# A two-stream attention block: the scale weight in two column chunks, the value rows in single key tiles, the last blocks of the value product moved

## The chip, the cores and the metric

The kernel runs on one core of a Trainium2 chip. The time is the device time in microseconds (us) of one execution. TensorE (PE in the profile) multiplies and transposes, and its weight loads are listed apart as PEld; VectorE (DVE), ScalarE (ACT) and GpSimd (POOL) work elementwise; SyncE (SP) issues most of the loads, and 16 DMA engines carry them out. The core's own work runs in program order on each engine, and the engines wait for one another through semaphores.

## The reference

Two streams of tokens, image (2 batches of 256) and text (2 of 32), with a model width of 1152, are normed, modulated by a vector `c`, projected to query, key and value, attended to together, projected and gated. Everything is bfloat16 at the borders.

```python
mod_i = (silu(c) @ wmod_img).reshape(B, 6, 1, D)     # the same for the text stream
shi, sci, gai = mod_i[:, 0], mod_i[:, 1], mod_i[:, 2]
hi = layernorm(x_img) * (1 + sci) + shi
qkvi = hi @ wqkv_img                                 # query, key, value
...
p = softmax(einsum('bqd,bkd->bqk', q, k) * D ** -0.5)
a = einsum('bqk,bkd->bqd', p, v)
out_i = x_img + gai * (a[:, Nt:] @ wo_img)
out_t = x_txt + gat * (a[:, :Nt] @ wo_txt)
```

What matters here is the first stage: the norm of the image tokens, the factor `1 + sci`, the value part of `hi @ wqkv_img`, and the shift `shi`.

## The kernel before

The width of 1152 is nine tiles of 128, called kt. The 512 image tokens are four blocks of 128, called i or x0 to x3; x0 and x1 belong to batch 0, x2 and x3 to batch 1. All engines follow the order in which the program is written: the schedule is manual, so an instruction that waits holds up everything behind it on its engine.

**Loads.** SyncE issues, in this order, the token blocks (`load_x`, L90) and the two weight matrices of the stage in chunks (`load_sc`, L94, and `load_v`, L98). The scale weight `w_sc_i` is cut by output columns, in chunks of 2, 2, 2 and 3 tiles (`KC`, L49): a chunk holds all 1152 rows of 256 or 384 columns, so that each piece of a row in a load is 512 or 768 bytes. The value weight `w_v_i` is cut by rows, in the same groups of kt, with whole rows of 2304 bytes. Behind these come the shift weight `w_sh_i` and the query weight `w_q_i`.

**Start.** TensorE runs 11 matmuls on zeros (`warm`, L127) while the first loads arrive. VectorE norms each block (`stats_of`, `std_of`, `out_of`; the square root between them is ScalarE's, L160). TensorE transposes the normed block in nine steps (`x_transposes`, L172) into two PSUM tiles, and ScalarE copies these to `hT_i`, the transposed tokens: plain copies (`evac_low`, `evac_high`) for the kt whose factor is not there yet, and copies multiplied with the factor (`evac_scaled`, L181) for those whose factor is.

**The factor.** `mod_scale` (L198) multiplies one column chunk of the scale weight with `silu(c)`: nine matmuls of two columns for each of its tiles. ScalarE or VectorE adds 1 and writes `mod_i`. For the kt that were copied without the factor, `apply_mod` (L208) multiplies `hT_i` in place on VectorE (0), GpSimd (1) or ScalarE (2).

**The value product.** `v_part` (L229) adds one chunk of kt to one accumulator: one block i and one half of 512 of the first 1024 value columns. Seven of the eight accumulators are open at once, in the seven PSUM banks of the pool `ps_mm`, which the transposes also use; an eighth bank is the pool `ps_sm`. Chunk 0 of all blocks comes first, then chunk 1, 2 and 3, with the transposes of x2 and x3 and the factors of chunks 1 to 3 between them. After the last chunk an accumulator is copied to `v_i` by `evac`, which takes VectorE and ScalarE in turn.

**The end of the stage.** `v_rest` (L336) computes the last 128 value columns for two blocks, once for x2, x3 and once for x0, x1. `rows_for_cols` (L369, with `strip_rows`, L357) multiplies the shift weight with `silu(c)` into four strips of rows; `select_cols` and `cols_out` turn these into columns. The eighth accumulator (x3, columns 512 to 1023; L390 to L395) is computed around this: four of its matmuls ahead of `select_cols` and five behind it. Then `apply_mod` adds the shift to `hT_i` in place (L397 to L399), and the query products start (`qk_img`, L441). The shift must come behind all the value products, because these use `hT_i` without it.

Of the kernel before, what the change touches and what calls it, by code (L numbers as in the profile page):

```python
# [14 lines left out]
def kernel(  # L15
# [33 lines left out]
    KC = [(0, 2), (2, 4), (4, 6), (6, KT)]  # L49
# [42 lines left out]
    def load_sc(ch):  # L92
        k0, k1 = KC[ch]
        nc.sync.dma_start(w_sc_i[:, :, k0 * P:k1 * P], w_view(wmod_img)[:, :, D + k0 * P:D + k1 * P])  # L94

    def load_v(ch):
        k0, k1 = KC[ch]
        nc.sync.dma_start(w_v_i[:, k0:k1, :], w_view(wqkv_img)[:, k0:k1, 2 * D:3 * D])  # L98
# [3 lines left out]
    load_sc(0)  # L102
    load_x(2)
    load_v(0)
    load_x(3)
    for ch in range(1, len(KC)):
        load_sc(ch)
        load_v(ch)
# [63 lines left out]
    def x_transposes(i, n0=5):  # L172
        tps = (ps_mm.tile([P, n0, P], bf, tag="mm", name="tp"),
               ps_mm.tile([P, KT - n0, P], bf, tag="mm", name="tp") if n0 == 5 else
# [6 lines left out]
    def evac_scaled(i, tps, n):  # L181
        for kt in range(n):
# [3 lines left out]
    def evac_low(i, tps, n):  # L186
        nc.scalar.copy(hT_i[:, n:tps[2], i * P:(i + 1) * P], tps[0][:, n:tps[2], :])
# [4 lines left out]
    def mod_cols(wt, out_ps, j0, j1):  # L192
        for j in range(j0, j1):
            for kt in range(KT):
                nc.tensor.matmul(out_ps[:, j - j0, :], lhsT=wt[:, kt, j * P:(j + 1) * P], rhs=sT[:, kt, :],
                                 start=(kt == 0), stop=(kt == KT - 1))

    def mod_scale(ch, eng, own=True):  # L198
        k0, k1 = KC[ch]
        pool, tag = (ps_sm, "sm") if own else (ps_mm, "mm")  # L200
        mps = pool.tile([P, KT, B], f32, tag=tag)
        mod_cols(w_sc_i, mps, k0, k1)
        if eng == "dve":
            nc.vector.tensor_scalar_add(mod_i[:, KT + k0:KT + k1, :], mps[:, 0:k1 - k0, :], 1.0)
        else:
            nc.scalar.activation(mod_i[:, KT + k0:KT + k1, :], mps[:, 0:k1 - k0, :], ACT.Identity, bias=1.0)
# [22 lines left out]
    def v_part(i, half, ch):  # L229
        k0, k1 = KC[ch]  # L230
        if ch == 0:
# [7 lines left out]


    def v_block(units, chs):
        for ch in chs:
            for (i, half) in units:
                v_part(i, half, ch)

    warm(4)
    silu_c()
    warm(7)
# [10 lines left out]

    stats_of(0, 0, NCH)  # L260
# [5 lines left out]
    evac_low(0, tps, 2)  # L266
# [42 lines left out]
    for (i, half) in SEVEN[:4]:  # L309
        v_part(i, half, 2)  # L310
# [532 lines left out]
```

## Time and profile before

| | us |
|---|---|
| median of 3 runs | 117.31 (117.13 to 117.89) |
| span of the profiled execution, first to last instruction | 115.8 |
| the median less that span | 1.5 |
| first scale matmul (L195) starts | 7.68 |
| first value matmul (L235) starts | 9.95 |
| last scale chunk's matmuls start | 20.26 |
| first query matmul (L450) starts | 32.47 |
| TensorE busy over the span | 110.6 |

Only the span of the profiled execution is known, not its time outside; the table sets the median beside it. In the profile, a line such as `L235 PE MATMUL va<-w_v_i,hT_i ... x63` names the source line, the engine, the operation, what is written from what, and how many instructions. The chain of waits follows the end of the kernel back, step by step, to what released each step. A time to landing counts from the issue of a load on its queue to the arrival of its last byte. A busy TensorE is not a TensorE at its peak, since matmuls overlap; where pace matters, the distance between starts is used. The granted clock is full throughout.

### The profile page before, as it was taken

How to read it: one execution, taken by the hardware profiler on the slowest of the kernel's cores; microseconds unless marked ns; L12 is line 12 of the kernel's file. 1: busy time of each engine (PE TensorE's matmuls, PEld its weight loads, DVE VectorE, ACT ScalarE, POOL GpSimd, SP SyncE). 2: the span in 40 equal slices, each digit the busy share in tenths (PEclk: the TensorE clock that was granted, in tenths of full speed). 3: DMA queues.
4: the chain of work that ended last, by engine and by line, in shares of the span. 5: the costliest groups of instructions: out<-in, count | busy, mean ns of one | idle time of the engine just before them, and what ended most of it. 6: DMA issues, size and time to landing. Idle time of an engine off the chain costs nothing.

```text
span 115.8 us, 2947 instructions
## 1 busy us (share of the span) xinstructions
PE 110.6 (96%) x1262; PEld 65.3 (56%) x1262; DVE 53.7 (46%) x138; ACT 34.2 (30%) x83; POOL 24.0 (21%) x55
## 2 busy tenths in 40 slices
PE   5978999999999999999999999999999999999990
PEld 1344563548644444486444445987677665568570
DVE  1689920354290312211572332136665804994771
ACT  4548660343270320121080121116455700000200
POOL 4000103660050000002215000000240300999000
PEclk9999999999999999999999999999999999999999
DMA  3999999999999999999999999999999999982052
GB/s 83 297 338 359 376 385 399 409 412 415 404 408 408 413 412 400 414 410 294 375 404 411 396 376 381 404 412 402 412 408 405 404 416 410 409 297 108 6 187 68
DMA packets 22840, 40.89 MB, mean 353 GB/s; under 512 B 1183, under 2 KB 6699, under 8 KB 22827
## 3 DMA queue, kind: packets, MB, share of 16 engines
q1 hardware_dynamic: 22032, 39.82, 91.8%
q0 software_dynamic: 480, 0.73, 1.7%
q8 instruction: 10, 0.16, 0.5%
q10 hardware_dynamic: 315, 0.14, 0.5%
q14 instruction: 3, 0.02, 0.1%
HBM read 39.36 MB, written 1.34 MB: 351 GB/s over the span
## 4 chain that ended last, share of the span: by engine, by line
PE 80%; SPq 9%; DMA 8%; issue 1%; DVE 1%
PE qkps L450 30%; PE ps L762 15%; DMA w_sc_i<-in_wmod_img_dram 8%; PE va L235 5%; SPq L98 5%; PE aps L671 5%; PE ps L507 4%; PE sps L531 4%; PE gps L361 4%; SPq L90 3%; PE ops L783 2%; PE ps L395 2%; PE ps L340 2%; PE ps L603 2%; SPq L94 1%; PE gps L423 1%
## 5 line engine op out<-in xcount | busy, mean ns | idle before, releaser
L450 PE MATMUL qkps<-hT_i,t 128*128 128x512 bf16 x162 | 35.6, 379 | 0.0
L450 PEld LDWEIGHTS <-t 128*128 128x128 bf16 x162 | 15.6, 98 | 18.6
L762 PE MATMUL ps<-t,aT 128*128 128x384 bf16 x99 | 16.4, 326 | 0.0
L762 PEld LDWEIGHTS <-aT 128*128 128x128 bf16 x117 | 11.1, 98 | 6.7 <-issue 0.2
L235 PE MATMUL va<-w_v_i,hT_i 128*128 128x512 bf16 x63 | 14.6, 379 | 0.2 <-ACT hT_i L183 0.2
L746 POOL TENSOR_TENSOR w_og<-t,gb 128x384 bf16<-128x384 bf16 x9 | 8.7, 996 | 6.1 <-DMA gb<-mod_scratch 6.1
L235 PEld LDWEIGHTS <-hT_i 128*128 128x128 bf16 x63 | 5.8, 97 | 6.8 <-ACT hT_i L190 0.3
L768 DVE TENSOR_TENSOR tmp<-ps,gb 128x384 bf16<-128x384 f32 x11 | 6.0, 549 | 4.9 <-DMA gb<-mod_scratch 4.2
L434 DVE TENSOR_SCALAR qkT<-qkps 128x512 bf16<-128x512 f32 x4 | 2.8, 692 | 11.4 <-PE qkps L450 11.4
L153 DVE BATCH_NORM_STATS2 stats<-x_i 128x6 f32<-128x384 bf16 x12 | 6.0, 542 | 2.6 <-DMA x_i<-in_x_img_dram 2.6
L130 PE MATMUL wps<-wz 128*128 128x512 bf16 x14 | 5.9, 574 | 1.2 <-DVE wz L120 1.2
L436 ACT ACTIVATE qkT<-qkps 128x512 bf16<-128x512 f32 x5 | 2.9, 596 | 13.6 <-PE qkps L450 13.6
L144 DVE CAST qkT<-qkps 128x512 bf16<-128x512 f32 x4 | 2.8, 692 | 6.7 <-PE qkps L450 6.7
L219 POOL TENSOR_SCALAR hT_i<-hT_i,mod_img 128x256 bf16<-128x256 bf16 x5 | 2.5, 510 | 16.1 <-ACT rstd L160 9.6
L146 ACT CAST qkT<-qkps 128x512 bf16<-128x512 f32 x5 | 2.8, 582 | 9.7 <-PE qkps L450 9.7
L558 POOL DMA_DIRECT2D mod_scratch<-g_sb x2 | 1.2, 583 | 20.7 <-ACT g_sb L556 20.7
L769 DVE TENSOR_TENSOR o<-tmp,x_i 128x384 bf16<-128x384 bf16 x11 | 5.2, 471 | 0.4
L684 DVE TENSOR_SCALAR aT<-aps,sv 128x288 bf16<-128x288 f32 (+2 forms) x11 | 4.3, 456 | 2.3 <-PE aps L671 2.3
L507 PEld LDWEIGHTS <-t 128*128 128x128 bf16 x162 | 4.9, 98 | 0.2
L507 PE MATMUL ps<-hT_t,t 128*128 128x64 bf16 x162 | 4.9, 193 | 0.0
L738 ACT CAST gbf_full<-bps 128x288 bf16<-128x288 f32 x2 | 0.7, 402 | 14.2 <-PE bps L736 14.2
L671 PE MATMUL aps<-pT,v_i 128*128 128x288 bf16 (+2 forms) x44 | 4.8, 264 | 0.1
(156 smaller groups left out, 139.8 us busy)
## 6 DMA issues: line engine op xcount, KB each, us to landing
t<-in_wmod_img_dram SPq DMA_DIRECT2D x2, 2592.0 KB, 19.3
t<-in_wqkv_img_dram SPq DMA_DIRECT2D x6, 864.0 KB, 13.8
t<-in_wqkv_txt_dram SPq DMA_DIRECT2D x2, 2592.0 KB, 18.4
t<-in_wmod_txt_dram SPq DMA_DIRECT2D x2, 1440.0 KB, 15.0
t<-in_wqkv_txt_dram SPq DMA_DIRECT2D x3, 864.0 KB, 16.0
t<-in_wmod_txt_dram SPq DMA_DIRECT2D x1, 2592.0 KB, 19.5
t<-in_wo_txt_dram SPq DMA_DIRECT2D x3, 864.0 KB, 15.3
t<-in_wmod_txt_dram SPq DMA_DIRECT2D x2, 1152.0 KB, 16.2
```

The costliest lines, as they stand in the source:

```text
L98: nc.sync.dma_start(w_v_i[:, k0:k1, :], w_view(wqkv_img)[:, k0:k1, 2 * D:3 * D])
L130: nc.tensor.matmul(ps[:], lhsT=wz[:, 0:P], rhs=wz[:], start=True, stop=True)
L153: nc.vector.bn_stats(stats[0:np_, k, :], x_ap[:, k * CH:(k + 1) * CH])
L235: nc.tensor.matmul(ps[:], lhsT=hT_i[:, kt, i * P:(i + 1) * P], rhs=w_v_i[:, kt, half * VW:(half + 1) * VW], start=(kt == 0), stop=(kt == K ...
L361: nc.tensor.matmul(gps[32 * g:32 * g + 32, 0:RC], lhsT=lhs[:, kt, :], rhs=wt[:, kt, g * RC:(g + 1) * RC], start=(kt == 0), stop=(kt == KT ...
L450: nc.tensor.matmul(pss[j - j0][:], lhsT=wq[:, kt, j * P:(j + 1) * P], rhs=hT_i[:, kt, :], start=(kt == 0), stop=(kt == KT - 1))
L507: nc.tensor.matmul(ps[:, j - j0, :], lhsT=wq[:, kt, j * P:(j + 1) * P], rhs=hT_t[:, kt, :], start=(kt == 0), stop=(kt == KT - 1))
L671: nc.tensor.matmul(bank[:, off:off + c1 - c0], lhsT=lhsT, rhs=rhs, start=(first[id(bank)] == n), stop=(final[id(bank)] == n))
L746: nc.gpsimd.tensor_mul(w_og[:, dt, 0:CH], w_o_i[:, dt, NG0:D], gb[:, B - 1, NG0:D])
L762: nc.tensor.matmul(ps[:, 0:cw], lhsT=aT[:, dt, t0:t0 + P], rhs=rhs, start=(dt == DTS[0]), stop=(dt == DTS[-1]))
L768: nc.vector.tensor_mul(tmp[:, 0:cw], ps[:, 0:cw], gb[:, b, cs])
L769: nc.vector.tensor_add(o[:, cs], tmp[:, 0:cw], x_i[:, i, cs])
```

## The change

The scale weight is now cut into two column chunks, of 4 and 5 tiles, and each chunk is loaded in two halves by rows (5 and 4 kt), so that a piece of a row is 1024 or 1280 bytes. The value weight is loaded in pieces of 1, 1, 2, 1, 2 and 2 kt instead of 2, 2, 2 and 3. There are 14 loads in this stage instead of 12.

`mod_half` runs the matmuls of one half of a chunk; two halves add up in one PSUM tile, and `mod_out` adds 1. The first chunk gives the factor of kt 0 to 3 at once, so `evac_scaled` covers four kt of each block, and only kt 4 to 8 are multiplied in place later, all in one go behind the second chunk. The square roots of x2 and x3 stand behind three scaled copies of the block before. `v_rows` runs the value matmuls kt by kt, both halves of a block together: kt 0 and 1 of x0 now come ahead of the transposes of x1, kt 2 and 3 of x0 and kt 0 and 1 of x1 ahead of those of x2, and so on. One warm-up pair stands between the two halves of the first chunk, one behind it (four instead of three in all). The last five kt are run unit by unit at the end.

At the end of the stage, the eighth accumulator is computed whole and copied out ahead of the shift rows; the narrow block of x2, x3 comes between the shift rows and `select_cols`, and that of x0, x1 behind `cols_out`, with its copy to `v_i` behind the shift.

```diff
-    KC = [(0, 2), (2, 4), (4, 6), (6, KT)]
+    KA = 4
+    KC = [(0, KA), (KA, KT)]
+    KH = [(0, 5), (5, KT)]
...
+    def load_sc(ch, half):
+        c0, c1 = KC[ch]
+        k0, k1 = KH[half]
+        nc.sync.dma_start(w_sc_i[:, k0:k1, c0 * P:c1 * P], w_view(wmod_img)[:, k0:k1, D + c0 * P:D + c1 * P])
+
+    def load_v(k0, k1):
         nc.sync.dma_start(w_v_i[:, k0:k1, :], w_view(wqkv_img)[:, k0:k1, 2 * D:3 * D])
 
     load_x(0)
     load_x(1)
-    load_sc(0)
+    load_sc(0, 0)
+    load_sc(0, 1)
+    load_v(0, 1)
     load_x(2)
-    load_v(0)
+    load_v(1, 2)
     load_x(3)
-    for ch in range(1, len(KC)):
-        load_sc(ch)
-        load_v(ch)
+    load_v(2, 4)
+    load_sc(1, 0)
+    load_sc(1, 1)
+    load_v(4, 5)
+    load_v(5, 7)
+    load_v(7, KT)
...
+    def mod_half(ch, half):
+        c0, c1 = KC[ch]
+        k0, k1 = KH[half]
+        if half == 0:
+            mod_ps[ch] = ps_sm.tile([P, KT, B], f32, tag="sm", name="mps")
+        for kt in range(k0, k1):
+            for j in range(c0, c1):
+                nc.tensor.matmul(mod_ps[ch][:, j - c0, :], lhsT=w_sc_i[:, kt, j * P:(j + 1) * P], rhs=sT[:, kt, :],
+                                 start=(kt == 0 and j == c0), stop=(kt == KT - 1 and j == c1 - 1))
...
+    def v_rows(i, k0, k1, halves=(0, 1)):
+        for kt in range(k0, k1):
+            for half in halves:
+                v_part(i, half, kt, kt + 1)
...
     tps = x_transposes(0)
     stats_of(1, 1, NCH)
-    evac_low(0, tps, 2)
+    evac_high(0, tps)
     std_of(1)
-    mod_scale(0, "act")
-    evac_scaled(0, tps, 2)
-    evac_high(0, tps)
+    mod_half(0, 0)
+    warm(2)
+    mod_half(0, 1)
+    mod_out(0, "act")
+    evac_scaled(0, tps, 0, KA)
     out_of(1)
-    warm(3)
+    warm(2)
+    v_rows(0, 0, 2)
     tps = x_transposes(1)
     stats_of(2, 0, NCH)
-    evac_scaled(1, tps, 2)
+    evac_scaled(1, tps, 0, 3)
     std_of(2)
-    evac_low(1, tps, 2)
+    evac_scaled(1, tps, 3, KA)
     evac_high(1, tps)
     stats_of(3, 0, 1)
     out_of(2)
-    v_block([(0, 0), (0, 1), (1, 0), (1, 1)], [0])
+    v_rows(0, 2, KA)
+    v_rows(1, 0, 2)
     tps = x_transposes(2, KT - 1)
     stats_of(3, 1, NCH)
-    evac_scaled(2, tps, 2)
+    evac_scaled(2, tps, 0, 3)
     std_of(3)
...
+    evac_scaled(2, tps, 3, KA)
     evac_high(2, tps)
+    evac_low(2, tps)
     out_of(3)
+    v_rows(1, 2, KA)
+    v_rows(2, 0, 2)
     tps = x_transposes(3, KT - 1)
     evac_high(3, tps)
+    evac_scaled(3, tps, 0, KA)
+    evac_low(3, tps)
+    v_rows(2, 2, KA)
+    mod_half(1, 0)
+    mod_half(1, 1)
+    mod_out(1, "dve")
+    for kt in range(*KC[1]):
+        apply_mod(kt, 0, TPB, False, 0 if kt < KT - 1 else 2)
+        apply_mod(kt, TPB, NIT, False, 1 if kt < KT - 1 else 2)
+    v_rows(3, 0, KA, (0,))
     v_i = act.tile([P, NIT, D], bf, tag="A")
...
+    for (i, half) in [(i, half) for i in range(NIT) for half in range(2)][:7]:
+        v_part(i, half, KA, KT)
...
-    v_rest(TPB, NIT)
-    v_rest(0, TPB)
+    ps = ps_mm.tile([P, VW], f32, tag="mm")
+    for kt in range(KT):
+        nc.tensor.matmul(ps[:], lhsT=hT_i[:, kt, 3 * P:4 * P], rhs=w_v_i[:, kt, VW:NM], start=(kt == 0), stop=(kt == KT - 1))
+    evac(v_i[:, 3, VW:NM], ps[:])
     shr = rows_for_cols(w_sh_i, "shr")
     cps = ps_sm.tile([P, NCOL + B], f32, tag="sm")
-    ps = ps_mm.tile([P, VW], f32, tag="mm")
-    for kt in range(KT):
-        if kt == 4:
-            select_cols(shr, cps)
-            cols_out(mod_i[:, 0:KT, :], cps, 0.0)
-        nc.tensor.matmul(ps[:], lhsT=hT_i[:, kt, 3 * P:4 * P], rhs=w_v_i[:, kt, VW:NM], start=(kt == 0), stop=(kt == KT - 1))
+    v_rest_out(TPB, NIT, v_rest(TPB, NIT))
+    select_cols(shr, cps)
+    cols_out(mod_i[:, 0:KT, :], cps, 0.0)
+    vr = v_rest(0, TPB)
...
-    evac(v_i[:, 3, VW:NM], ps[:])
+    v_rest_out(0, TPB, vr)
```

## The prediction

> **What bounds the kernel now.** I read the page's chain first, then the chain of waits of the first 33 us, then the timelines of TensorE and ScalarE there, and last the load issues one by one.
>
> ```profile
> span 115.8 us, 2947 instructions
> ...
> PE 80%; SPq 9%; DMA 8%; issue 1%; DVE 1%
> ```
>
> And the chain in order of time (start, length, what ran):
>
> ```profile
> 11.42 8.79 DMA w_sc_i<-in_wmod_img_dram
> 20.21 0.05 issue
> 20.26 0.83 PE mps L195 x27
> 21.09 6.00 PE va L235 x27
> 27.09 2.01 PE ps L340 x36
> 29.09 1.10 PE gps L361 x36
> ...
> 32.47 17.48 PE qkps L450 x81
> ```
>
> From 20.26 us on the chain is TensorE almost without a break. Whatever moves the start of the query products (32.47 us) moves the end equally; no later wait on a load would absorb it. The span is 115.8 us; the median of the runs, 117.31, is 1.5 us more, which I carry unchanged.
>
> The chain names a DMA until 20.21 us, but that overstates the loads: TensorE was working until just before, by its timeline (start, length, engine, line, what):
>
> ```profile
> 9.10 0.68 PE L178 MATMUL tp<-ident,xn_i 128*128 128x128 bf16 x9 [0.15 <-DVE xn_i L165]
> 9.95 1.89 PE L235 MATMUL va<-w_v_i,hT_i 128*128 128x512 bf16 x8 [0.17 <-ACT hT_i L183]
> 11.90 0.68 PE L178 MATMUL tp<-ident,xn_i 128*128 128x128 bf16 x9
> 12.41 0.59 PE L195 MATMUL mps<-sT,w_sc_i 128*128 128x2 bf16 x18
> ...
> 16.58 3.61 PE L235 MATMUL va<-w_v_i,hT_i 128*128 128x512 bf16 x16
> ```
>
> Steady prices: 16 value matmuls in 3.61 us, of which the last is pipeline: 0.217 each (27 in 6.00 later: 0.222); nine transposes 0.52 before the next may start (11.90 to 12.41); a scale matmul 0.026 (18 in 0.59). From 9.10 TensorE had 27 transposes (1.6), 63 value matmuls (13.7), 63 scale matmuls (1.6), 36 narrow ones (2.1), the shift rows (1.3), and the last wide block with its selection (2.2): 22.5 us, so 31.6; the end was 32.47, so all waits in this stretch are below 0.9 us. That is the most that better loads can win.
>
> **The loads** (x0 to x3 are the four token blocks, value row k the k-th 128 rows of the value weights). Issue plus time to landing, one load at a time: x1 lands at 4.5 us, scale chunk 0 at 7.7, x2 at 8.3, value chunk 0 at 9.8, x3 at 10.6, scale 1 at 12.2, scale 2 at 15.3, scale 3 at 20.2, value 3 at 22.3. Two of the answers (scale chunk 0 and value 3; the last column is us to landing):
>
> ```profile
> w_sc_i<-in_wmod_img_dram SPq DMA_DIRECT2D x1, 576.0 KB, 6.0
> ...
> w_v_i<-in_wqkv_img_dram SPq DMA_DIRECT2D x1, 864.0 KB, 10.4
> ```
>
> From 7.7 to 22.3 us 5.31 MB landed. The 3.25 MB with 2304-byte rows take 7.9 us at the 411 GB/s of the stretch 22 to 24 us, which leaves 6.7 us for 2.06 MB of short scale rows (512 and 768 bytes): 306 GB/s. The new scale rows are 1024 and 1280 bytes; their rate lies between 306 and 411, and I take 360, the middle. At 306 GB/s chunk 0 should take 1.9 us behind x1; it took 3.2. This opening lag of 1.25 us is still 1.0 at scale 1 and 0.7 at scale 2 by the same sums.
>
> New order after x1 (0.59 MB at 4.5): scale half 0 (0.655 MB) and half 1 (0.524), 3.3 us at 360; then value row 0, x2, value row 1, x3, 0.72 us each at 411, and value rows 2-3, 1.44. With the lag: scale halves **7.4 and 8.8**, value row 0 9.6, x2 10.3, value row 1 **11.0**, x3 11.8, value rows 2-3 **13.0**; the second scale chunk about 17, the last value rows 21.1. For 13.0 the ends are 12.1 (no lag) and 13.4 (lag 1.0, rate 330). The two extra issues take SyncE 0.43 each (as at 1.65 us), ahead of all later weights; they cost nothing, since later issues stand on a full queue anyway (3.32 us for the one at 8.05). Were the queue empty, they would cost 0.9.
> The Trainium skill (DMA: Bandwidth & Descriptors, "Why small descriptors are slow") gives a fixed overhead of about 3 cycles per packet beside 32 bytes a cycle. As an estimate from that page the longer rows would run near 400 GB/s, and value rows 2-3 would land 0.3 us earlier. The trace agrees only in direction (306 against 411 for 512/768 against 2304 bytes).
>
> **Part by part, in TensorE's order.** Transposes of x0 stay at 6.76. The first scale half: 20 x 0.026 from 7.4, to 7.9; two warm matmuls to 8.4; the second half waits for 8.8, then 16 x 0.026, 9.2. Now 36 scale matmuls instead of 18 lie ahead of everything else, and so does the whole first chunk. From the last scale matmul's issue (8.14) to the first scaled tile (8.89) the old timeline has 0.75 us through ScalarE: value row 0 of x0 can start at 9.95 (the two warm matmuls lie inside). Two matmuls, 10.4.
> Next comes value row 1, not there until 11.0: 11.1 with its receipt, to 11.5. **Behind these two matmuls wait the transposes of x1**, whose input is ready near 9.4 (out of VectorE at 9.0 before, 0.3 later as the copy ahead of the square root is 640 columns wide, some 0.7 us by 0.61 for 512). They ran at 9.10 before and now run at 11.5 to 12.05: 2.4 us later, and with them all ScalarE work on x1 to x3.
> Value rows 2-3 for x0 wait for 13.0: 13.1 to 13.95; value rows 0-1 for x1, 14.8; transposes of x2, 14.8 to 15.35 (11.90 before; their input is ready at about 14.0, so not the limit).
>
> ScalarE's timeline around x2 and x3, from which their prices come:
>
> ```profile
> 12.56 0.62 ACT L183 ACTIVATE hT_i<-tp,mod_img 128x128 bf16<-128x128 bf16 x2 [0.67 <-PE tp L178]
> 13.08 0.29 ACT L160 ACTIVATE rstd<-mv,eps_t 128x1 f32<-128x1 f32 x1
> 13.28 0.78 ACT L187 COPY hT_i<-tp 128x768 bf16<-128x768 bf16 x1
> 13.96 0.27 ACT L190 COPY hT_i<-tp 128x128 bf16<-128x128 bf16 x1
> ...
> 15.62 1.15 ACT L183 ACTIVATE hT_i<-tp,mod_img 128x128 bf16<-128x128 bf16 x4
> ```
>
> Each scaled copy costs ScalarE 0.26 (12.56 to 13.08 for two). Behind x2's transposes there are now three before the square root of x3, and the rest after it: start 0.66 after the transposes (15.5), square root 16.3 to 16.55, then VectorE, 0.86 (11.03 to 11.89 before): input of x3 at 17.4. ScalarE finishes the eight-tile bank of x2 at 17.65. Six accumulators are then open in seven banks, so the transposes of x3 need that bank: 17.7, where TensorE, with eight more matmuls, is ready at 17.1. They end at 18.25; four matmuls 19.1; 45 scale matmuls (their chunk landed at 17) 20.3. ScalarE is done with x3 2.5 us after its transposes begin (14.76 to 17.24 before), 20.2, which frees the seventh accumulator's bank. Four matmuls: 21.2.
> The second chunk's scaling is five tiles at once instead of 2, 2 and 3: VectorE 4 x 0.24, POOL 4 x 0.48, ScalarE 2. It starts near 20.5 under those four matmuls and stays ahead: x0 and x1 need a tile each 0.22, x2 only 4.3 us later. Without that cover it would cost about 1 us (the VectorE four). The last value rows (21.1) are there too, with 0.7 us to spare before the fourth of the five tiles.
> Then 35 value matmuls at 0.221, 28.9; the wide block 2.05, 31.0; shift rows 1.26, 32.25; narrow block 1.0, selection 0.13, narrow block 1.0: **34.4**. The moved blocks are the same matmuls. The shift matrix landed at 28.7 (issue 14.51 plus 14.2) and its rows began at 29.0 without a wait, so putting 2 us of work ahead of them removes none. The filler behind the selection shrinks from five wide matmuls, 1.1 us, to 1.0; the shift itself on tiles 0-1 must wait for the last reader there, so the first query matmul may start 0.1 later: 34.5. Evacuations change engines in pairs, beside TensorE.
> Against 32.47 that is **+2.0 us**: 119.3. The same by waits: about 0.75 for the first scaling, 0.7 for value row 1, 1.05 for value rows 2-3, 0.6 at x3, 0.1 at the end, less the old waits and the 18 scale matmuls already done.
>
> **Rivals.**
> *The loads keep ahead* (not slower). If the opening lag was the short rows' own doing, value row 1 lands by 10.4 and value rows 2-3 by 11.8. Then: scaling at 9.55, the transposes of x1 at 10.4, x2's at 13.0 (three scaled copies, square root, VectorE), x3's at 15.9 by the bank, seventh accumulator 18.5, end 32.7: 117.5. For it: 257 GB/s in 4 to 6 us, when chunk 0 moves. Against: x2 and value 0, long rows, carry the same lag on. It decides from 11.8 us for value rows 2-3; between that and 13.0 the end moves about one for one. Even this has no gain, since ScalarE's chain then binds; without any wait after the first scaling TensorE would end at 31.7, 116.5.
> *The clock falls.* TensorE is idle about 2.5 us in pieces between 7.9 and 13.1. Seven warm matmuls from 3.17 us took 3.17, twice the later pace, so there is a slow state; as much work in it again, 3.2 us, would cost 1.6: 120.9. Against: the old gaps of 6 to 10 us (1 us idle in 4) left it at full pace.
> The Trainium skill (TensorE: Matmul & The Clock Gate, "HAM oscillation") puts the fall at idle gaps over about 3.4 us; the longest here is 1.1, so by that page it does not come.
> *Each load pays by itself.* Two more loads on the queue. x2 landed 0.65 us behind scale 0 and x3 0.8 behind value 0, which is their bytes' time; a charge of, say, 0.3 on each of the six loads from scale half 1 to value rows 2-3 would cost 1.8 more: 121.1.
>
> **How the numbers follow.** Forecast (118.5 to 120.3) 0.68; loads ahead (116.6 to 118.4) 0.17; clock 0.08; a charge per load 0.04; something unseen that gives over 1% 0.03. A measurement of this kernel tells about 1%, 1.2 us. Range: 12.1 instead of 13.0 gives 118.4; 13.4, an x3 chain 0.3 longer and 0.3 less of an overlap give 120.3; to leave out no more than 0.2 I take 118.0 to 120.5. Slower by over 1% 0.80, within 0.17, faster 0.03.
>
> **What would show it.** Transposes of x1 behind the first four value matmuls near 11.5, of x2 near 14.8, of x3 near 17.7; waits of weight loads on the value rows at 10.4 and 12; the shift rows near 31.0 and the query products at 34.5; nothing but a shift after that. I am wrong if value rows 2-3 land by 12, if the transposes don't wait in order, or if a later stage gives the time back.

## The result and the profile after

The changed kernel takes **120.85 us** (median of four runs, 120.69 to 120.91) against 117.6 us (117.13 to 118.05) for the kernel before in the same session: a ratio of 1.027, with a 95% interval of 1.023 to 1.031. The forecast was 119.3, with a range up to 120.5. The sign was right, the loss was some 1.6 times as large as forecast: the span grew by 3.3 us, not by 2.0.

The page of the changed kernel, its span, the busy share of TensorE in 40 slices of about 3 us, the granted clock in the same slices, and the shares of the chain that ended last:

```profile
span 119.1 us, 2940 instructions
...
PE   5828899999999999999999999999999999999990
...
PEclk9998599999999999999999999999999999999999
...
PE 84%; DMA 6%; SPq 2%; ACT 2%; DVE 2%; issue 1%
```

All of the difference but the last tenths arises in the first twelve slices, before the query products. In the third slice (6 to 9 us) TensorE is busy for only two tenths, and in the fifth the clock is at half, which the kernel before does not show anywhere. TensorE's timeline there (start, length, line, what, and in brackets the idle time before and what ended it):

```profile
8.76 0.65 PE L208 MATMUL mps<-sT,w_sc_i 128*128 128x2 bf16 x20 [1.44 <-DMA w_sc_i<-in_wmod_img_dram]
...
10.12 0.55 PE L208 MATMUL mps<-sT,w_sc_i 128*128 128x2 bf16 x16 [0.25 <-DMA w_sc_i<-in_wmod_img_dram]
...
11.34 1.53 PE L245 MATMUL va<-w_v_i,hT_i 128*128 128x512 bf16 x3 [0.22 <-ACT hT_i L190]
13.09 1.17 PE L185 MATMUL tp<-ident,xn_i 128*128 128x128 bf16 x9 [0.22 <-DVE stats L160]
14.39 1.95 PE L245 MATMUL va<-w_v_i,hT_i 128*128 128x512 bf16 x8
16.18 0.67 PE L185 MATMUL tp<-ident,xn_i 128*128 128x128 bf16 x9
...
18.84 0.66 PE L185 MATMUL tp<-ident,xn_i 128*128 128x128 bf16 x9 [0.27 <-ACT hT_i L194]
```

The order of events is the forecast one: scale halves, value rows 0 and 1 of x0, transposes of x1 behind them, value rows 2-3, transposes of x2, transposes of x3 behind a bank that ScalarE gives back. But everything sits 1.1 to 1.6 us later than forecast. By issue plus time to landing, the scale halves landed at 8.75 and 10.0 us (forecast 7.4 and 8.8), value row 0 at 10.7 (9.6), value row 1 at 12.2 (11.0), value rows 2-3 at 14.35 (13.0). The issues of the second scale half (at 2.12 us) and of value rows 2-3 (at 6.35 us), with the time to landing last:

```profile
w_sc_i<-in_wmod_img_dram SPq DMA_DIRECT2D x1, 512.0 KB, 7.9
...
w_v_i<-in_wqkv_img_dram SPq DMA_DIRECT2D x1, 576.0 KB, 8.0
```

The value matmuls at 14.39 carry no bracket, and the chain of waits puts two scaled copies of x1 in front of them, which end at 14.40. The first of those matmuls read only x0, whose copies were long done; what fits is the load that landed at 14.35. The copies ended in the same moment by chance, and the transposes, at half clock, had filled the time until then.

The stretches of one microsecond show both troubles at once. Columns: the stretch, its length, busy time and count on TensorE, its weight loads, VectorE, ScalarE and GpSimd; then granted clock, DMA share, GB/s:

```profile
5.00:6.00 1.00, 0.40 (x2) 0.00 (x0) 0.94 (x4) 0.29 (x1) 0.00 (x0) 1.00 0.88 228
...
12.00:13.00 1.00, 0.87 (x2) 0.26 (x2) 0.97 (x3) 0.06 (x1) 0.00 (x0) 0.50 1.05 399
```

While the first scale chunk is on its way the queue moves 228 GB/s, and between 4 and 7 us 224 in the mean; by 12 us it moves some 400, and there the clock is at half. The kernel before moved 262 in 4 to 7 us.

The bytes in all show something else. From the landing of x1 to that of the first scale chunk, first in the kernel before and then in the changed kernel, with the same columns:

```profile
4.46:7.63 3.17, 2.56 (x14) 0.92 (x12) 3.10 (x8) 0.98 (x3) 0.00 (x0) 1.00 0.99 284
...
4.95:10.07 5.12, 2.23 (x34) 1.12 (x31) 3.48 (x10) 1.18 (x3) 0.00 (x0) 1.00 0.97 317
```

At 284 GB/s the first stretch moved 0.90 MB, though the scale chunk has 0.59; at 317 GB/s the second moved 1.62 MB, and its chunk has 1.18. The rest belongs mostly to loads that stand behind the chunk in the queue. What moved between the landings of the two scale halves of the changed kernel (8.71 to 10.07 us):

```profile
DMA packets 304, 0.55 MB, mean 405 GB/s; under 512 B 29, under 2 KB 94, under 8 KB 304
```

Only 65 of these 304 packets have the size of a scale row (512 bytes to 2 KB); 210 are longer, rows of tokens and value weights. A load has landed only with its last byte, and here the queue ran at 405 GB/s for later loads while the last scale rows were still missing.

The chain of the changed kernel, at the hand-over to the query products and at its end (start, length, what):

```profile
35.38 0.38 PE qkps L454
...
110.12 5.88 PE ps L766 x45
116.01 0.02 issue
116.03 0.29 DVE o L769
```

The query products start at 35.38 us against 32.47 before, +2.9. From the end of the last addition (116.32) to the end of the span it is 2.78 us; before, the last addition ended at 113.37 and 2.43 us followed. Start of the query products +2.9, first query products +0.16 (17.64 us for the 81 matmuls against 17.48), end +0.35, all else −0.1: the 3.3 us of the span.

### The profile page after: what moved, and what is told of

Same layout as the page of the kernel before. It is cut to its first block, busy times and chain, and to the rows that moved or that the text cites. A ratio compares the mean times of both kernels' runs of the same rounds, so it can differ in the third digit from the quotient of the medians.

```text
span 119.1 us, 2940 instructions
## 1 busy us (share of the span) xinstructions
PE 110.6 (93%) x1257; PEld 65.8 (55%) x1263; DVE 52.5 (44%) x133; ACT 35.0 (29%) x87; POOL 23.6 (20%) x54
## 4 chain that ended last, share of the span: by engine, by line
PE 84%; DMA 6%; SPq 2%; ACT 2%; DVE 2%; issue 1%
PE qkps L454 30%; PE ps L766 15%; PE va L245 9%; DMA x_i<-in_x_img_dram 6%; PE aps L675 5%; PE ps L511 4%; PE sps L535 4%; PE gps L365 3%; PE ops L787 2%; PE ps L341 2%; PE ps L607 2%; PE ps L392 2%; ACT hT_i L190 1%; PE tp L185 1%; DVE stats L160 1%; PE gps L427 1%
## 5 line engine op out<-in xcount | busy, mean ns | idle before, releaser
L137 PE MATMUL wps<-wz 128*128 128x512 bf16 x15 | 5.3, 487 | 1.2 <-DVE wz L127 1.2
L190 ACT ACTIVATE hT_i<-tp,mod_img 128x128 bf16<-128x128 bf16 x16 | 4.8, 370 | 2.9 <-PE tp L185 2.9
L230 POOL TENSOR_SCALAR hT_i<-hT_i,mod_img 128x256 bf16<-128x256 bf16 x4 | 2.0, 518 | 18.1 <-DVE mod_img L215 18.1
L151 DVE CAST v_i<-va 128x512 bf16<-128x512 f32 x4 | 2.8, 692 | 5.2 <-PE va L245 5.2
## 6 DMA issues: line engine op xcount, KB each, us to landing
t<-in_wmod_txt_dram SPq DMA_DIRECT2D x2, 1440.0 KB, 14.8
t<-in_wmod_txt_dram SPq DMA_DIRECT2D x1, 2592.0 KB, 18.8
```

The source lines that it names most:

```text
L137: nc.tensor.matmul(ps[:], lhsT=wz[:, 0:P], rhs=wz[:], start=True, stop=True)
L151: nc.vector.tensor_copy(out_ap, in_ap)
L190: nc.scalar.activation(hT_i[:, kt, i * P:(i + 1) * P], tps[0][:, kt, :], ACT.Identity, scale=mod_i[:, KT + kt, i // TPB:i // TPB + 1])
```

## The experiments

Edits are shown against the changed kernel or the kernel before, as each heading says. Times are medians, with the ratio to the kernel before of the same session and its 95% interval; where no interval is given, the kernel ran once, with a profile.

### 1. Was it the clock? Six more warm matmuls (changed kernel)

```
+    warm(6)
     mod_half(0, 0)
```

> The changed kernel with six more warm-up matmuls ahead of the first scale half, where TensorE waited from 7.3 to 8.8 us. If the loads and the order make the time (theory 1): the granted clock stays at full from 11.4 to 14.8 us, but value rows 2-3 still land at 14.35 us, so the query products start at 35.0 instead of 35.4, and the time is 120.4 against 120.85. If the clock is the story (theory 2): 3.4 us at half pace cost up to 1.7, so 119.2.

121.2 us (120.97 to 122.03), 1.030 [1.022, 1.038]. The granted clock stayed at full throughout, and the time did not fall. TensorE's timeline of this run:

```profile
12.24 0.66 PE L185 MATMUL tp<-ident,xn_i 128*128 128x128 bf16 x9
14.02 1.89 PE L245 MATMUL va<-w_v_i,hT_i 128*128 128x512 bf16 x8 [1.11 <-ACT hT_i L190]
```

The transposes of x1 run 0.85 us earlier than in the changed kernel, and then TensorE stands 1.1 us until value rows 2-3 (landed at 13.9). The half clock of the changed kernel lay in front of a wait and was mostly paid out of it: the seventh accumulator begins at 20.94 instead of 21.38. Even those 0.4 us didn't reach the end, by the chain of this run:

```profile
11.73 10.98 DMA w_v_i<-in_wqkv_img_dram
...
22.76 7.07 PE va L245 x32
```

The last value rows landed at 22.7 and held the value matmuls. They had landed at 21.7 in the changed kernel, so part of this wait is the scatter of landings between executions. In all four executions the clock stayed up, and none was faster than 120.97 us: **the half clock is not what makes the 3.3 us**. By the seventh accumulator it cost at most 0.4 us in the profiled execution; the loads stand behind it at two places.

### 2. Is it the order on TensorE? Transposes ahead of the late value rows (changed kernel)

```
+    tps = x_transposes(1)
     v_rows(0, 0, 2)
-    tps = x_transposes(1)
     stats_of(2, 0, NCH)
...
-    v_rows(0, 2, KA)
     v_rows(1, 0, 2)
     tps = x_transposes(2, KT - 1)
+    v_rows(0, 2, KA)
     stats_of(3, 1, NCH)
```

> The changed kernel with the transposes of x1 ahead of the value matmuls of x0, and those of x2 ahead of value rows 2-3 of x0, same loads. If the order behind late loads matters (theory 1): transposes of x1 near 10.6 instead of 13.1, of x2 near 14.2 instead of 16.2, of x3 near 17 instead of 18.8, query products near 34, time 119.4. If only the landings matter, value rows 2-3 at 14.35 set the pace of everything and the time stays at 120.8. If the clock matters (theory 2), it falls here too and the gain is below 0.5.

120.51 us (119.93 to 120.73), 1.021 [1.015, 1.027]. Timeline:

```profile
11.40 1.17 PE L185 MATMUL tp<-ident,xn_i 128*128 128x128 bf16 x9
...
14.53 0.68 PE L185 MATMUL tp<-ident,xn_i 128*128 128x128 bf16 x9
```

The transposes of x1 come 1.7 us earlier and those of x2 1.65, the query products 1.1 (34.30), and the span of the profiled run is 1.0 shorter. The medians differ less, by 0.3, with overlapping intervals. Some of the loss seems to be the order; most of it is not. The normed x2 was ready only at 14.47, just ahead of its transposes: x2 landed at 11.56 (8.3 before), with 1.18 MB of scale rows and a value row ahead of it.

### 3. Is the end of the stage free? The new tail alone (kernel before)

```
-    v_rest(TPB, NIT)
-    v_rest(0, TPB)
+    ps = ps_mm.tile([P, VW], f32, tag="mm")
+    for kt in range(KT):
+        nc.tensor.matmul(ps[:], lhsT=hT_i[:, kt, 3 * P:4 * P], rhs=w_v_i[:, kt, VW:NM], start=(kt == 0), stop=(kt == KT - 1))
+    evac(v_i[:, 3, VW:NM], ps[:])
     shr = rows_for_cols(w_sh_i, "shr")
...
+    v_rest_out(TPB, NIT, v_rest(TPB, NIT))
+    select_cols(shr, cps)
+    cols_out(mod_i[:, 0:KT, :], cps, 0.0)
+    vr = v_rest(0, TPB)
```

> The kernel before with only the end of the stage changed (wide block ahead of the shift rows, narrow blocks behind them). Theory 1: the same matmuls in another order; the shift on x0 and x1 may hold the first query matmul for 0.1 us, so 117.6 to 117.8, no difference that can be measured. If the end of the stage is a part of the loss (theory 3): 118.1 or more, with a gap ahead of the query products.

117.78 us against 117.81, 1.002 [0.998, 1.006]: nothing that can be measured. Its chain shows a small price all the same, the first query products 0.16 longer than before, as in the changed kernel:

```profile
32.01 17.64 PE qkps L453 x81
```

### 4. The other way round: value rows ahead of the scale rows (changed kernel)

```
-    load_sc(0, 0)
-    load_sc(0, 1)
     load_v(0, 1)
...
     load_v(2, 4)
+    load_sc(0, 0)
+    load_sc(0, 1)
```

> The changed kernel with the value rows 0 to 3 and x2, x3 loaded ahead of all scale loads; a slow kernel, run only for its landings. If the opening is slow whatever is loaded: 220 to 270 GB/s from 4 to 7 us again, value rows 2-3 land near 11.3. If the scale rows' first reads are slow: near 400 GB/s from 4 us, value rows 2-3 near 9.5, and the scale halves behind them take 5 us instead of 3.3. Time 122 to 124 either way.

124.45 us. Value rows 2-3 land at 10.2 now, but the scale halves at 11.9 and 13.3, nothing can be scaled before, and the clock lies at half from 8.5 to 18.8 us. With wide rows in the opening the queue moved 300 GB/s in 4 to 7 us. From 10 to 13 us it moved nothing but scale rows, at 389 GB/s. So the opening is slow with wide rows too, and the same scale rows are not slow later.

### 5. The order of loads and the order on TensorE, in the kernel before

One edit sends the second scale chunk ahead of x2 and value chunk 0, so that 1.18 MB or so of scale rows come first as in the change; one puts x0's value matmuls ahead of the transposes of x1; one does both.

```
     load_sc(0)
+    load_sc(1)
     load_x(2)
     load_v(0)
     load_x(3)
-    for ch in range(1, len(KC)):
+    load_v(1)
+    for ch in range(2, len(KC)):
```

> The kernel before with one load moved: the second scale chunk (0.59 MB) ahead of x2 and value chunk 0, so that as many scale bytes lie ahead of the value rows as in the changed kernel. Nothing else changes. If the load order is the main cause: value chunk 0 lands near 11.3 us instead of 9.8, the first value matmul starts there, the transposes of x2 near 13.1 instead of 11.9, and the query products 1.1 later, 118.9. If the order of TensorE's work is the main cause, most of this is taken up by later slack: 117.8 to 118.2.

```
+    v_block([(0, 0), (0, 1)], [0])
     tps = x_transposes(1)
...
-    v_block([(0, 0), (0, 1), (1, 0), (1, 1)], [0])
+    v_block([(1, 0), (1, 1)], [0])
```

> The kernel before with one move on TensorE: the four value matmuls of x0 (chunk 0) ahead of the transposes of x1, as in the changed kernel. Loads as before. If the order is the main cause: transposes of x1 near 10.9 instead of 9.1, the value matmuls of x1 then wait for ScalarE until 12.0, transposes of x2 near 13, query products 1.1 later, 118.9. If the loads are, the move costs 0.3 or less: 117.8 to 118.1.

> The kernel before with both moves together: second scale chunk ahead of x2 and value chunk 0, and the value matmuls of x0 ahead of the transposes of x1. If loads and order act together as in the changed kernel: transposes of x1 near 12.2, value matmuls of x1 near 13.5, transposes of x2 near 14.4, query products near 35, 120.1 to 120.4. If the two overlap (both only wait for the same landing): no more than the larger of the two alone, 118.9.

Loads alone: 119.75 us (118.62 to 120.45), 1.014 [1.008, 1.020]. Order alone: 118.13, 1.007 [1.004, 1.011]. Both: 121.87, 1.036 [1.029, 1.042]. So the two parts together, in the old chunks and without the new tail, lose about as much as the change does or more. They also lose more than the sum of what each loses alone (1.4% and 0.7%), but this does not show that they make each other worse: the profiled run with both edits lies at half clock for two stretches, 9.4 to 16.2 us, and by their mean clock (0.968 to 0.971) two more executions do too. At 1.25 us a stretch (below), an estimate from these runs, the clock alone would make up most of the excess. In the run with the loads alone one line carries the wait:

```profile
11.68 3.22 PE L237 MATMUL va<-w_v_i,hT_i 128*128 128x512 bf16 x8 [2.03 <-DMA w_v_i<-in_wqkv_img_dram]
```

Eight value matmuls take 3.22 us, against 1.89 before, as the clock fell here too (at half from 11.0 to 14.4 us). The four executions of this kernel give the price of such a stretch when it lies on the path. Two at full clock took 118.62 and 119.41, two with a mean clock of 0.986 (one stretch of 3.4 us at half) took 120.10 and 120.45: 1.26 us between the means, of two executions each.

### 6. Short rows again, new order kept (changed kernel)

```
-    load_sc(0, 0)
-    load_sc(0, 1)
+    for c0 in (0, 2):
+        nc.sync.dma_start(w_sc_i[:, :, c0 * P:(c0 + 2) * P], w_view(wmod_img)[:, :, D + c0 * P:D + (c0 + 2) * P])
```

> The changed kernel with its first scale chunk loaded as two pieces by columns (all 1152 rows, 512-byte pieces of rows) instead of two halves by rows (1024-byte pieces); same bytes, same order of everything else. If the opening is slow whatever is loaded: 220 to 260 GB/s from 4 to 7 us again and the whole chunk landed near 10.2, some 0.3 later than in the changed kernel by the shorter rows. If the changed kernel's way of reading causes the lag: 260 GB/s or more and the chunk landed near 9.3. The first half of the chunk now needs both pieces, so TensorE starts the factor only then; time 120.8 to 121.5.

122.08 us. The stretch 4 to 7 us moved 265 GB/s, against 224 in the changed kernel, and the whole chunk landed near 9.6 instead of 10.0. But now already the first matmuls of the chunk need both pieces, so TensorE begins later, the clock lies at half for two stretches, and the query products start at 36.58. The size of the rows is then not what makes the opening slow: the shorter rows were no slower here. They were hardly faster either: x1 landed at 4.4 us instead of 4.95, and from there to the whole chunk it is 5.2 us (5.1 in the changed kernel).

### 7. The changed kernel once more

> The changed kernel once more, to see how much of its start differs between executions. If a lag of the opening loads is its own: value rows 2-3 land between 13.7 and 14.4 us again, the granted clock falls to half for one window near 11 to 15 us in most executions, time 120.5 to 121.2. If the first profile was an exception: landings near 13.0, clock at full, 119.5.

121.03 us (120.49 to 122.09), 1.031 [1.024, 1.038]; here too the first scale half landed at 8.95, the second at 10.3, value rows 2-3 at 14.6, at 217 GB/s in 4 to 7 us. Executions with one stretch at half clock took 120.59 and 120.49, those with two 121.48 and 122.09: 1.25 us between the means for the second stretch, the price seen in experiment 5.

### 8. Clock held and the last load's wait removed; and the order on top (changed kernel)

```
+    warm(6)
     mod_half(0, 0)
...
-    for (i, half) in [(i, half) for i in range(NIT) for half in range(2)][:7]:
-        v_part(i, half, KA, KT)
+    for (k0, k1) in ((KA, 7), (7, KT)):
+        for (i, half) in [(i, half) for i in range(NIT) for half in range(2)][:7]:
+            v_part(i, half, k0, k1)
```

> The changed kernel with six more warm-up matmuls ahead of the first scale half and with the last five key tiles run in two passes over the seven accumulators (4 to 6, then 7 and 8), so that the last value rows are needed 4.6 us later. If in the run with the warm-up matmuls alone the gain of the full clock was lost to the last value rows, which landed at 22.7 us there: no wait ahead of that point, query products near 34.7 and 120.3. If the clock costs nothing: 121 again.

The next run adds the order of experiment 2.

> The two edits of the run before (warm-up matmuls, last five key tiles in two passes) and the transposes of x1 and x2 ahead of the value matmuls that wait for later loads. If order, clock and last value rows are all that the change loses besides its larger first scale chunk: transposes of x2 near 14.2, query products near 33.5, 119.0. What is left above 117.6 is then the larger first chunk and x2, which lands 3 us later than before. If the order gains nothing once the clock is held: 120.3.

120.71 us (1.027 [1.021, 1.033]) and 120.09 (1.021 [1.014, 1.027]), both at full clock. Holding the clock and splitting the last pass together give 0.1 to 0.3 against the two medians of the changed kernel, which is within their scatter; the order gives 0.6 more, with overlapping intervals. One line of TensorE's timeline in the second:

```profile
13.55 0.68 PE L185 MATMUL tp<-ident,xn_i 128*128 128x128 bf16 x9 [0.76 <-DVE xn_i L172]
```

With all three mended, x2's transposes still run at 13.55 instead of 11.90, and the wait before them is for the normalised x2, whose tokens landed at 10.6. None of these versions beats the kernel before.

### 9. Does the landing explain the miss? The first chunk from another place (changed kernel)

```
-    load_sc(0, 0)
-    load_sc(0, 1)
+    for (k0, k1) in KH:
+        nc.sync.dma_start(w_sc_i[:, k0:k1, 0:KA * P], w_view(wqkv_img)[:, k0:k1, D:D + KA * P])
```

> The changed kernel with its first scale chunk read from another matrix (the key columns of the query-key-value weight, whose rows lie 6912 bytes apart instead of 13824), so its factor for key tiles 0 to 3 is not the reference's; same pieces, sizes and order. If the distance between the rows makes the opening slow: 290 GB/s or more from 4 to 7 us and the chunk landed near 9. If not: 210 to 250 GB/s and 9.6 to 10.1, as before. Time 120.0 or 120.9.

> The changed kernel with its first scale chunk read from the key columns of the query-key-value weight (rows 6912 bytes apart), now timed; its factor for key tiles 0 to 3 is not the reference's. If the late first chunk is what the prediction missed: chunk landed near 8.8, clock at full or nearly, 119.3 to 119.7, that is 2 us above the kernel before instead of 3.3. If the single look before was a lucky execution: 120.5 to 121.

The rows keep their 1024 bytes but lie 6912 bytes apart instead of 13824. In the first run the queue moved 290 GB/s in 4 to 7 us, the chunk landed at 8.8 and value rows 2-3 at 13.1: by luck almost the landings that the forecast had assumed (8.8 and 13.0). The scale values are others here, but the shapes and the order of the work are the same. Its timeline:

```profile
8.90 0.55 PE L208 MATMUL mps<-sT,w_sc_i 128*128 128x2 bf16 x16 [0.64 <-DMA w_sc_i<-in_wqkv_img_dram]
...
11.50 0.66 PE L185 MATMUL tp<-ident,xn_i 128*128 128x128 bf16 x9
13.19 1.89 PE L245 MATMUL va<-w_v_i,hT_i 128*128 128x512 bf16 x8 [1.03 <-DMA w_v_i<-in_wqkv_img_dram]
14.91 0.67 PE L185 MATMUL tp<-ident,xn_i 128*128 128x128 bf16 x9
...
17.58 0.66 PE L185 MATMUL tp<-ident,xn_i 128*128 128x128 bf16 x9 [0.27 <-ACT hT_i L194]
```

Forecast were 11.5, 13.1, 14.8 and 17.7. The span was 117.8 us, the time 119.61. This is the cleanest reading of the study: given the forecast landings, the forecast order of waits follows to about 0.1 us, up to the transposes of x3. That the whole span equals the forecast is luck: the query products started at 34.12, 0.4 earlier than forecast, and the longer end took this back. Timed, the kernel took 120.22 (119.88 to 120.91), 1.023 [1.017, 1.029]. In its profiled execution the chunk landed at 9.1. Three of the four executions show a stretch at half by their mean clock (0.983 to 0.986); two of them took 120.57 and 120.91 us, but the third took 119.88, no longer than the one at full clock. So the price of a stretch is not the same everywhere.

Two more sources were meant to tell whether the distance of the rows is what matters.

```
+        nc.sync.dma_start(w_sc_i[:, k0:k1, 0:KA * P], w_view(wmod_txt)[:, k0:k1, D:D + KA * P])
```

> The same, read from the scale columns of the text stream's modulation weight: another matrix, rows again 13824 bytes apart (factor again not the reference's). If the distance between the rows makes the opening slow: 200 to 250 GB/s from 4 to 7 us, chunk landed at 9.6 to 10.1, 120.5 to 121. If it is the one matrix or its place: as with the other source, 290 GB/s, 8.8, 119.5.

```
+        nc.sync.dma_start(w_sc_i[:, k0:k1, 0:KA * P], w_view(wo_img)[:, k0:k1, 0:KA * P])
```

> The same, read from the output weight, whose rows lie 2304 bytes apart (factor again not the reference's). If the distance is the cause and the effect grows with it: at least as good as 6912, 290 GB/s or more, chunk landed at 8.8 or earlier, 119.0 to 119.6. If 6912 was good for another reason: 9.6 to 10.1 again.

At the same distance in another tensor: 257 GB/s, chunk at 10.0, value rows 2-3 at 14.3, 120.71 us (1.025 [1.020, 1.030]), as in the changed kernel. At 2304 bytes: 292 GB/s, but the chunk landed only at 9.9, 120.74 us. The same distance gives the same lateness, but the closest rows are not the earliest. With these the queue moved as much in 4 to 7 us as with the 6912-byte distance, but by the time the chunk landed it had moved 0.8 MB beyond the loads up to that chunk, against 0.46 in the first run above. **Why the opening is slow, and how much of the later loads moves first, is not settled.**

### 10. Does a load cost something by itself? (kernel before)

Two more loads, by sending value chunks 2 and 3 in two pieces each; two fewer, and seven fewer, by sending later weights in one piece.

```
-        nc.sync.dma_start(w_v_i[:, k0:k1, :], w_view(wqkv_img)[:, k0:k1, 2 * D:3 * D])
+        for (a, b) in ((k0, k0 + 1), (k0 + 1, k1)) if ch >= 2 else ((k0, k1),):
+            nc.sync.dma_start(w_v_i[:, a:b, :], w_view(wqkv_img)[:, a:b, 2 * D:3 * D])
```

> The kernel before with its last two value chunks loaded in two pieces each, so two loads more and nothing else changed. From the end of the last addition to the end of the span the kernel before has 2.43 us, the changed kernel 2.78. If each load more costs time behind the last store: 2.78 here too, span 116.1 to 116.3. If the longer end of the changed kernel is something else: 2.43.

```
-    w_sh_t = load_w(wmod_txt, 0, K2)
-    w_sc_t = load_w(wmod_txt, D, K2)
+    w_sh_t = load_w(wmod_txt, 0)
+    w_sc_t = load_w(wmod_txt, D)
```

> The kernel before with the text stream's shift and scale weights loaded in one piece each instead of two: two loads fewer. If each load costs some 0.17 us behind the last store: 2.1 us from the last addition to the end of the span and 117.2 against 117.5. If not: 2.43 and no difference.

The third makes the same edit also to w_v_t, w_o_i and w_o_t.

> The kernel before with five later weights (text shift, scale and value, both output weights) loaded in one piece each: seven loads fewer. If each load costs some 0.17 us behind the last store: 1.2 us from there to the end of the span, 116.3 to 116.6, unless a weight needed by its first part now comes late, which would show as a wait of TensorE for a weight. If not: 117.5.

Two more: 118.87 us. Two fewer: 117.72, 1.004 [1.002, 1.007]. Seven fewer: 118.17, 1.006 [1.004, 1.009]. Fewer loads are not faster, which speaks against a charge on each. The end of the kernel with two more loads:

```profile
114.03 0.29 DVE o L766
```

Its span is 117.1, so 2.78 us follow the last addition: exactly as in the changed kernel, with none of its other edits. To the hundredth, the changed kernel and its variants, with 14 loads of tokens, scale and value weights, show 2.76 to 2.78 in twelve profiled runs; the five kernels with the 12 loads of before show 2.41. So **the 0.35 us at the end come with the two loads**. It is no price per load, though: with two fewer than before 2.52 us follow the last addition, with seven fewer 2.82.

The trace shows what counts there. After its last store SyncE runs nine waits, in the same order in every run, which take 0.06 us each when nothing holds them up. They are for semaphores, eight of which the loads and stores use in turn. The last store lands 1.5 us after the last addition in every run. In the kernel before, the wait for it is the ninth and ends at 1.55. In the changed kernel it is the third, ends at 1.53, and six more follow, to 1.90. With two more loads it is the third as well, with two fewer the seventh, with seven fewer the second. So the number of loads sets the place of that wait, and the change lost 0.35 us there by chance.

The rest of the first run's loss, 1.0 us at the start of the query products, goes with a stretch at half clock from 9.1 us and a late first chunk, both before any split load lands: with an opening that is the same, the first scale chunk was used at 8.26 instead of 7.68 here (7.29 with seven fewer), so that landing scatters by half a microsecond either way between executions.

## Why the prediction was right and where it was wrong

**What bounds the kernel: right.** A later start of the query products moved the end by as much, and no wait behind it gave anything back (the chain's later part is 0.1 shorter).

**Order and waits on TensorE: right.** The transposes of x1 stood behind value row 1, those of x2 behind value rows 2-3, those of x3 behind ScalarE's bank. Experiment 9 shows the sum itself, from landings to transposes, good to 0.1 us; experiments 2 and 8 put the in-order part at 0.3 to 0.6 us of the loss by the medians, which is within their scatter, and at 1.0 by the profiled span of experiment 2.

**The landings: here it failed.** The step that failed is the landing of the first scale chunk: 3.3 us at 360 GB/s and an opening lag of 1.0, 4.3 us behind x1, with every later load behind it by the same lag. Measured were 5.1 us (4.95 to 10.07). At 360 GB/s that is a lag of 1.8, and all of it was there when the first half landed, 3.76 us behind x1. From then on the sum was right: the second half came 1.36 us later (forecast 1.4) and value rows 2-3 another 4.3 (forecast 4.2). With x1 0.45 late in this execution, the chunk landed at 10.0 instead of 8.8 and value rows 2-3 at 14.35 instead of 13.0, beyond the range's 13.4. x1 is not needed for it: in the repeat it landed at 4.3, and value rows 2-3 at 14.6.

The reading behind that step failed too. It took the lag of the landings for a property of the opening that a new order inherits. It is mostly bytes of later loads that move first. In the kernel before the queue had moved 0.47 MB more than all loads up to its first chunk when that landed, and 0.36 to 0.42 more at x3 and scale 1; 0.41 MB at the 411 GB/s of the prediction is the lag of 1.0. In the changed kernel it was 0.73 MB at its first chunk and 0.68 at value rows 2-3. Over the first 13.0 us both kernels moved the same (282 and 284 GB/s), and the 3.69 MB of the changed kernel are more than the 3.54 MB up to value rows 2-3; these still waited, as part of what had moved stood behind them in the queue. As an estimate from these numbers, half of the 1.35 us (0.27 MB) is more bytes of later loads, and the other half is that by 13.0 us the queue had moved 0.27 MB less in all than the sum implies. The rate that the prediction gives the short rows, 306 GB/s, comes from the same landings and has the same fault. Why more of the later loads went first is not shown; it scatters, from 0.37 to 0.74 MB at value rows 2-3 in six profiled runs of this opening.

The new rows also gained nothing at this place: 212 to 252 GB/s in 4 to 7 us in those six runs, against 262 to 298 in eight with the 512-byte rows of before, and 4.8 to 6.0 us from x1 to the whole chunk, where the 512-byte rows of experiment 6 took 5.2. Later the same rows ran at 389 GB/s (experiment 4). The Trainium skill (DMA: Bandwidth & Descriptors, "Why small descriptors are slow") names a fixed overhead per packet, so that longer pieces run faster; the trace agrees with the prediction's estimate from it, near 400 GB/s, in that later stretch, and disagrees in the opening.

Of the 1.35 us, 0.9 reached the query products (35.38 against 34.5), since the steps from the transposes of x2 to the query products were 0.5 us shorter than summed (19.2 against 19.7).

**"The two extra issues ... cost nothing": half right.** They delayed no landing that can be seen, but with them came 0.35 us behind the last addition, by the place of one wait (experiment 10). **"Nothing but a shift after that"** missed this and the 0.16 us of the first query products, which the new tail brings (experiment 3; the forecast had 0.1 for it at their start). Landings 0.9, end 0.35, query products 0.16, less 0.1: the 1.3 us between the forecast and the profiled span.

**The tail: right.** 1.002 with an interval across 1.

**The rivals.** *The loads keep ahead* is refuted: they were later still, and at full clock TensorE stood 1.1 us for value rows 2-3 (experiment 1). *The clock falls* did happen, in all eight executions of the changed kernel, and 120.9 lies near the result; but that is luck. At full clock the kernel takes 121.2 or 120.7 (experiments 1 and 8), since that stretch lay in front of a load's wait. The executions of the repeat with a second stretch took 1.25 us more. The prediction had put the longest gap at 1.1 us; it was 1.44, and the clock fell all the same. Its reasoning was also incomplete: I took the old gaps as evidence against it, and the time it asks for is in the last section. *Each load pays by itself* is refuted for the opening by the changed kernel's own landings: the five loads from value row 0 to value rows 2-3, 1.77 MB, landed within 4.28 us behind the chunk, 410 GB/s, which leaves no room for 0.3 us each. At the end of the kernel the number of loads did cost time, but not by a price for each.

## What to carry to other kernels

A load has landed with its last byte, and in these traces 0.2 to 0.8 MB of the loads behind it had moved by then. So do not read a queue's rate or its lag off landings alone: add up all the bytes that moved up to a landing. A new order does not inherit the old lag, and the first load of a queue deserves a wide range: in these runs 0.59 MB took 2.5 to 3.8 us behind x1, and 1.18 MB 4.5 to 6.0. Every load behind it is late by the same amount. On an engine that works in order, list for each matmul group that may wait which independent instructions stand behind it; moving the transposes of the next block ahead may give back some of the loss, but a block whose tokens were pushed back in the queue waits anyway. A disturbance that lies in front of a wait, such as a slow clock here, is not worth mending before the wait is gone. And where a kernel's end is compared, look at the order of its last waits before blaming the change.

## What was not expected of the hardware

**The clock fell without a long gap.** The longest idle time of TensorE before the fall in the changed kernel was 1.44 us. What the ten profiled runs with a fall have in common is the 3.4 us before it: TensorE was busy for only 1.0 to 2.2 us of them, a good part of it with transposes and matmuls of two columns. Each stay at half lasted 3.4 us or a multiple (3.4, 6.8, 10.2). In the changed kernel the 3.4 us up to the fall at 11.14 held 2.11 us of work. With six more warm matmuls ahead of the first scale half they held 3.19 (experiment 1) and 2.98 (experiment 8), and the clock stayed up in all twelve executions of the three kernels that have them, and in none of the eight executions of the changed kernel. Little work does not always bring a fall: runs at full clock have stretches of 3.4 us with 1.6 to 1.8 us of work, and in the changed kernel itself 4.32 to 7.73 us held 1.75 and brought none. Why not is not shown. The Trainium skill (TensorE: Matmul & The Clock Gate, "HAM oscillation") speaks of idle gaps over about 3.4 us; these runs show falls that last 3.4 us or a multiple, and show that short gaps that add up to some 1.2 us or more in such a stretch can be enough.

**The opening of the queue.** In 4 to 7 us the queue moved 212 to 313 GB/s in all runs, later about 390 to 410. The 1024-byte rows ran at 212 to 252 there from the scale weight (six runs), 257 from another tensor with the same distance, 290 and 313 from a third with half the distance, and 292 at 2304 bytes; one or two runs each, so the cause is open. A faster opening did not always mean an earlier chunk, because loads behind it move at the same time.

**The end of the kernel** takes 2.41 to 2.82 us behind the last addition. SyncE's nine last waits come in a fixed order, 0.06 us each, and it matters how many of them stand behind the one for the last store: none in the kernel before, six in the changed one.
